# Issuing the first block of K ahead of the first query weights in a two-layer decode kernel

## The chip, the cores and the metric

The kernel runs on one core of one Trainium2 chip. The metric is device time in microseconds (us) for one execution, and a comparison of two kernels uses the median of several executions. One further execution was taken by the hardware profiler; every duration below comes from that one. Engines are called by the names of the profile: PE is the matrix engine, PEld its weight loads, DVE the vector engine, ACT the scalar engine, POOL the general one. SP is the engine that issues nearly all loads here. "SPq" stands for its queue of instructions and "ACTq" for ACT's.

## What is computed

A decode step for one token: attention over a cached K and V of 4096 positions in 32 heads of 128, then an MLP of 512 to 1376 to 512, and the same two once more with the same weights and caches. All values are 32-bit floats.

```python
def _A_ref(x, k_cache, v_cache, wq, wo):
    q = (x @ wq).reshape(B, Sq, H, Dh).transpose(0, 2, 1, 3)
    scores = jnp.einsum("bhqd,bhkd->bhqk", q, k_cache) * (Dh ** -0.5)
    p = _softmax(scores, axis=-1)
    o = jnp.einsum("bhqk,bhkd->bhqd", p, v_cache)
    return o.transpose(0, 2, 1, 3).reshape(B, Sq, H * Dh) @ wo
...
x = A_x
x = x + _A_ref(_layernorm(x), A_k_cache, A_v_cache, A_wq, A_wo)
x = x + _B_ref(_layernorm(x), B_w1, B_b1, B_w2, B_b2)
x = x + _A_ref(_layernorm(x), A_k_cache, A_v_cache, A_wq, A_wo)
x = x + _B_ref(_layernorm(x), B_w1, B_b1, B_w2, B_b2)
```

K and V hold 67 MB each, far more than the on-chip memory, so both layers stream them from device memory. A little of the second layer's data is kept over from the first.

## The kernel before

**Tiles.** The 32 heads are taken in 8 groups of 4 (`G = 8`, counted by `g`). A group's K is one block of 128 partitions x 16384 floats, 8.39 MB, loaded as one DMA (in the last group of a layer in pieces), and so is its V. Each group also has query weights (wq) and output weights (wo) of 1.05 MB each, the two of neighbouring groups loaded as one pair of 2.1 MB.

**Memory.** One tile, `arena`, holds everything that is loaded. Three homes of a block each form a ring, `RING = (0, 16 * NC, 8 * NC)`, where `NC` is 2048 floats per partition: `A_AT` at 0, `B_AT` at `16 * NC`, `C_AT` at `8 * NC`. In the first layer K of group g goes to `RING[2 * g % 3]` and V to `RING[(2 * g + 1) % 3]`: K0 to A_AT, V0 to B_AT, K1 to C_AT, V1 to A_AT again. The very first wq has no place of its own: it lies at `SHARED`, which is inside the home of V0:

```python
KEPT_V = 26 * U
SHARED = B_AT + KEPT_V
...
wq_t = by_four(load(SHARED, of_w(1, 0, 1)))
```

A block spans 32 stretches of `U = 512` floats, and wq takes stretches 26 to 29 of B_AT. So V0's load overwrites the first wq, and has to wait until that wq has landed and PE has read it. The pairs of weights that follow have their own place, `PAIR`.

**Order.** All big loads go through `load()` (line 68), which issues them from SP and keeps them in the order in which the program names them. SP executes its instructions one after the other: a load that waits holds back every load behind it. PE's instructions are kept in program order in the same way by `matmul()` (line 73). Three small loads (x, b1, b2) are issued from ACT (lines 92 to 94).

**A group in the first layer** (lines 321 to 346): load K, 32 matmuls `scores` (each shown as two records in the profile), a softmax on DVE and ACT (`exponentials`), four transposes on PE (`weights`), load V, 32 matmuls `values`, load the next pair of weights, `head_out` (output projection) and `next_queries` (the next group's queries). Ahead of the loop, `first_queries` (line 296) computes the queries of group 0: four blocks of `query_block` read wq and x, with the mean and the variance of x (`mean_of`, `rstd_of`) worked out between them. The load of K0 stands in the loop, through `blocks` (line 288), and therefore behind that of wq.

**The rest.** After group 7 come the MLP, then the second layer, which begins with the blocks still on the chip (group 7, then V of group 6) and goes down to group 0, then the second MLP and the output.

Of the kernel before, what the change touches and what calls it, by code (L numbers as in the profile page):

```python
# [23 lines left out]
C = 8  # L24
# [5 lines left out]
NC = 4 * U  # L30
# [6 lines left out]
A_AT, B_AT, C_AT = RING  # L37
# [5 lines left out]
HALVES = ((0, 4), (4, 8))  # L43
# [7 lines left out]
def decode_layers(ctx: ExitStack, tc: tile.TileContext, x, k, v, w, w1, b1, w2, b2, out):  # L51
# [5 lines left out]
    def ctile(name, *shape):  # L57
        return const.tile([P, *shape], F32, name=name)
# [6 lines left out]
    def at(first, n):  # L65
        return arena[:, first : first + n]

    def load(first, src):
        t = at(first, src.shape[-1])
        tc.keep_in_program_order(nc.sync.dma_start(t, src))  # L70
        return t
# [4 lines left out]
    def quarters(first):  # L76
        return [at(first + U * j, U) for j in range(4)]

    def part(src, g, a, b):
        return src[g][:, NC * a : NC * b]  # L80

    def of_w(row, i, n):
        return w[row][:, NC * i : NC * (i + n)]

    def by_four(t):
        return t.rearrange("p (j n) -> p j n", j=4)


    wq_t = by_four(load(SHARED, of_w(1, 0, 1)))
    b1c, b2c = ctile("b1c", FB), ctile("b2c", 4)  # L90
    xcol = ctile("xcol", 4)
# [62 lines left out]
    def idle(to, n=U):  # L154
        matmul(to[:, :n], zero[:, 0:1].to_broadcast([P, P]), at(C_AT, n), start=True, stop=True)
# [34 lines left out]
    def scores(z, c, kt):  # L190
        for j in range(J):
            matmul(pS[32 * j : 32 * j + C, :], z[:, j, C - 1 - c : 2 * C - 1 - c], kt[j],
                   start=(c == 0), stop=(c == C - 1))

    def exponentials(sc, nsc):
        nc.vector.tensor_reduce(ml[:, 0:1], pS, axis=AX.X, op=ALU.max)  # L196
        mt, m, bias = small("mt", 32), small("m"), small("mt", 32)
        nc.vector.transpose(mt, ml)
        nc.vector.tensor_reduce(m, mt[:, :C], axis=AX.X, op=ALU.max)
        nc.vector.tensor_scalar(mb[:, :C], m.to_broadcast([P, C]), nsc, None, op0=ALU.mult)  # L200
        nc.vector.transpose(bias, mb)  # L201
        p = at(SCRATCH, U)
        nc.scalar.activation(p, pS, AF.Exp, bias=bias[:, 0:1], scale=sc, accum_out=ml[:, 0:1])  # L203
        return p

    def weights(p):
        for b in range(4):
            tc.keep_in_program_order(nc.tensor.transpose(  # L208
                pT[:, b].rearrange("p j r -> p (j r)"), p[:, P * b : P * (b + 1)], ident))
        pt = work.tile([P, P], F32, name="turned").rearrange("p (j c b) -> p j c b", j=J, c=C)  # L210
        nc.vector.tensor_copy(pt, pT[:, :, :, :C].rearrange("p b j c -> p j c b"))  # L211
        lt, l, lr, rl = small("mt", 32), small("l"), small("mt", 32), small("rl")
        nc.vector.transpose(lt, ml)  # L213
        nc.vector.tensor_reduce(l, lt[:, :C], axis=AX.X, op=ALU.add)
        nc.vector.tensor_copy(lb, l.to_broadcast([P, 32]))
        nc.vector.transpose(lr, lb)
        nc.vector.reciprocal(rl, lr[:, 0:1])
        return pt, rl

    def values(i, pt, vt, c):  # L220
        for j in range(J):
            matmul(pO[32 * j : 32 * j + 4, :], pt[:, j, c, :], vt[j],
                   start=(i == 0), stop=(i == C - 1))

    def head_out(rl, wt, last=False):
        ot = at(SCRATCH, U)
        nc.vector.transpose(ot, pO)  # L227
        o, on = small("o", 4), on_wide
        own = at(SCRATCH, 4 * 129).rearrange("p (b q) -> p b q", q=129)[:, :, :P]
        own = own.rearrange("p b (d q) -> p d b q", q=32)[:, :, :, 0]  # L230
        nc.vector.tensor_reduce(o, own, axis=AX.X, op=ALU.add)  # L231
        if last:
            nc.vector.tensor_scalar(on[:, :4], o, rl, None, op0=ALU.mult)
        else:
            nc.vector.tensor_scalar(in_quarters(on, 4), o.unsqueeze(1).to_broadcast([P, J, 4]), rl, None,  # L235
                                    op0=ALU.mult)
        for d in range(4):
            if last:
                for j in range(J):
                    matmul(pS[32 * j : 32 * j + 1, :P], on[:, d : d + 1], wt[:, d, P * j : P * (j + 1)],  # L240
                           start=(d == 0), stop=(d == 3))
            else:
                matmul(pO, on[:, d : d + P], wt[:, d, :], start=(d == 0), stop=(d == 3))
        return of_32(turned(pS) if last else turned(pO, wide=True), 4)
# [34 lines left out]
    def load_w1(first, a, b):  # L279
        load(first + W1C * a, w1[:, W1C * a : W1C * b])  # L280
# [4 lines left out]
    def in_rows(first, n, rows):  # L285
        return [at(first + n * i, n) for i in range(rows)]

    def blocks(src, g, home, pieces=((0, C),)):
        for a, b in pieces:
            load(home + NC * a, part(src, g, a, b))  # L290
            for c in range(a, b):
                yield c, quarters(home + NC * c)

# [14 lines left out]
    def next_queries(n, xs, negm, wt):  # L308
        for c in range(4):
            matmul(pO, xs[:, 2 * c : 2 * c + P], wt[:, c, :], start=(c == 0), stop=(c == 3))  # L310
        return queries(n, negm, wide=True)

    def add_up(acc, own):
        t = small("acc", 4)
        nc.vector.scalar_tensor_tensor(t, own, 1.0, acc, op0=ALU.mult, op1=ALU.add)
        return t
# [4 lines left out]
    for g in range(G):  # L321
        final = g == G - 1
        k_home, v_home = RING[2 * g % 3], RING[(2 * g + 1) % 3]
        for c, t in blocks(k, g, k_home, HALVES if final else ((0, C),)):
            scores(z, c, t)
        pt, rl = weights(exponentials(sc, nsc))
        for c, t in blocks(v, g, v_home, LAST if final else ((0, C),)):
            values(c, pt, t, c)
            if final and c > 4:
                idle(pS)  # L330
            if g == G - 2:
                for j in range(J):
                    i = 4 * c + j - KEPT_V // U
                    if i >= 0:
                        nc.scalar.copy(pK[i], t[j])
        if final:
            wo_t = by_four(load(PAIR, of_w(g % 2, g, 1)))
            for i in range(3):
                load_w1(SHARED, i, i + 1)
            own = head_out(rl, wo_t, last=True)  # L340
            load_w1(SHARED, 3, 4)
        else:
            pair = load(PAIR, of_w(g % 2, g, 2))
            acc = add_up(acc, head_out(rl, by_four(pair[:, :NC])))
            wq_t = by_four(pair[:, NC:])
            z = next_queries(g + 1, xs, negm, wq_t)
# [8 lines left out]
    g = G - 2  # L355
# [28 lines left out]
    for i, first in enumerate([C_AT + 30 * U, C_AT + 31 * U] + [PAIR + U * j for j in range(4)]):  # L384
        t = at(first, U)
# [11 lines left out]
    for n in range(2, G):  # L397
        g, final = G - 1 - n, n == G - 1
        k_home, v_home = homes[(2 * n - 1) % 3], homes[2 * n % 3]
        for c, t in blocks(k, g, k_home, HALVES if final else ((0, C),)):  # L400
            scores(z, c, t)
        pt, rl = weights(exponentials(sc, nsc))
        for c, t in blocks(v, g, v_home, LAST if final else ((0, 5), (5, 8)) if n == 2 else ((0, C),)):
            values(c, pt, t, c)
            if final and c > 4:
                idle(pS)
        if final:
            wo_t = by_four(load(PAIR, of_w(g % 2, g, 1)))
            for a, b in W1_AT_END:
                load_w1(A_AT, a, b)  # L410
            for a, b in W2_AT_END:
                load_w2(A_AT + 11 * U, a, b)
            own = head_out(rl, wo_t, last=True)
        else:
            pair = load(PAIR, of_w(g % 2, g - 1, 2))
            acc = add_up(acc, head_out(rl, by_four(pair[:, NC:])))
            z = next_queries(n + 1, xs, negm, by_four(pair[:, :NC]))
# [47 lines left out]
```

## Time and profile before

| | before |
|---|---|
| median of 3 runs | 681.27 us (680.49 to 681.55) |
| the profiled execution, its own time | 679.55 us |
| its span, first to last instruction | 677.8 us |
| mean granted TensorE clock | 0.841 |
| PE busy | 433.1 us, 64% |
| DVE busy | 110.7 us, 16% |
| ACT busy | 22.2 us, 3% |
| bytes read from device memory | 286.14 MB, 422 GB/s over the span |

1.75 us of the profiled execution lie outside its span. Two things help in reading the views that follow. The page's row of DMA gives, for 40 equal slices of the span (16.9 us each), the share of time in which the 16 DMA engines were moving data, in tenths, 9 being 90% or more. The view of windows gives the same for chosen stretches, but counts each packet whole in the stretch in which it begins. A packet here is one partition's row of a load, 64 KB for a block of K or V and 8 KB for the first wq, so that in short stretches the share can be far over 1 and be followed by 0.00 while the engines are still at work on what has begun.

### The profile page before, as it was taken

The page shows a single profiled execution, that of the slowest core. Times are in us where ns is not written, and L with a number is a line of the kernel's source. Part 1 is how long each engine was busy: PE and PEld are TensorE (multiplying, and loading weights), DVE is VectorE, ACT ScalarE, POOL GpSimd, SP SyncE. Part 2 cuts the span into 40 slices and gives each one's busy share as a digit, 9 for nine tenths or more (in the row PEclk, how much of TensorE's full clock was granted, in tenths as well). Part 3 has the DMA queues.
Part 4 walks back from the last instruction along what each step waited for, and adds up shares of the span by engine and source line. Part 5 has one row for each costly group of instructions (what it writes and reads, how often), then busy time and mean ns, then how long its engine had stood idle before and what let it go on. Part 6 is the DMA issues. An engine that isn't in the chain of part 4 may idle for free. (4 is left out here: it accounts for less than half of the span.)

```text
span 677.8 us, 6359 instructions
## 1 busy us (share of the span) xinstructions
PE 433.1 (64%) x2792; PEld 119.4 (18%) x2792; DVE 110.7 (16%) x431; ACT 22.2 (3%) x47; POOL 4.3 (1%) x21
## 2 busy tenths in 40 slices
PE   1547666485554874667777897686455764766776
PEld 0112112121111211111113222221111111211112
DVE  1012101111021101210212312211021011210211
ACT  0010000000000000001000110000000000000000
POOL 1000000000000000000000000000000000000000
PEclk9969768797698876977979998998698776977977
DMA  9999999999999999999999999899999999999997
GB/s 372 434 433 433 435 433 433 416 449 437 430 433 413 451 433 430 433 431 422 428 413 359 426 459 414 358 468 441 427 433 398 465 433 423 437 430 410 426 416 294
DMA packets 11404, 286.56 MB, mean 423 GB/s; under 512 B 1776, under 2 KB 1776, under 8 KB 3440
## 3 DMA queue, kind: packets, MB, share of 16 engines
q1 hardware_dynamic: 10944, 286.14, 98.7%
q8 instruction: 22, 0.36, 0.2%
q10 hardware_dynamic: 432, 0.01, 0.0%
q14 instruction: 6, 0.05, 0.0%
HBM read 286.14 MB, written 0.00 MB: 422 GB/s over the span
## 5 line engine op out<-in xcount | busy, mean ns | idle before, releaser
L74 PE MATMUL pO<-arena,turned 128*4 128x512 f32 x1024 | 144.8, 726 | 76.8 <-DMA arena<-in_v 75.6
L74 PE MATMUL pS<-arena,zq 128*8 128x512 f32 x1024 | 137.7, 698 | 70.8 <-DMA arena<-in_k 65.4
L74 PE MATMUL pO<-arena,x_wide 128*128 128x512 f32 (+1 forms) x176 | 54.9, 508 | 24.4 <-DVE turned L137 18.1
L74 PE MATMUL pO<-arena,on_wide 128*128 128x512 f32 x112 | 51.8, 605 | 18.6 <-DVE on_wide L235 18.6
L74 PEld LDWEIGHTS pS<-arena,zq 128*8 128x8 f32 x1024 | 29.1, 99 | 176.3 <-issue 167.1
L74 PEld LDWEIGHTS pO<-arena,turned 128*4 128x4 f32 x1024 | 27.6, 97 | 183.8 <-issue 179.5
L137 DVE STREAM_TRANSPOSE turned<-pO 32x128 f32<-32x128 f32 x112 | 35.0, 312 | 101.1 <-PE pO L74 99.9
L227 DVE STREAM_TRANSPOSE arena<-pO 128x512 f32<-128x512 f32 x16 | 11.5, 717 | 220.4 <-PE pO L74 220.4
L208 PE MATMUL pO<-ident,arena 128*128 128x128 f32 x64 | 14.5, 368 | 43.9 <-ACT arena L203 42.4
L196 DVE TENSOR_REDUCE ml<-pS 128x1 f32<-128x512 f32 x16 | 11.1, 692 | 185.0 <-PE pS L74 185.0
L74 PEld LDWEIGHTS pO<-arena,x_wide 128*128 128x128 f32 (+1 forms) x176 | 21.6, 155 | 57.1 <-DVE turned L137 26.5
L203 ACT ACTIVATE arena<-pS,mt,sc 128x512 f32<-128x512 f32 x16 | 12.4, 777 | 523.7 <-DVE mt L201 523.7
L74 PEld LDWEIGHTS pO<-arena,on_wide 128*128 128x128 f32 x112 | 20.1, 189 | 51.7 <-DVE on_wide L235 31.6
L208 PEld LDWEIGHTS pO<-ident,arena 128*128 128x128 f32 x64 | 9.3, 181 | 58.6 <-ACT arena L203 51.3
L74 PE MATMUL pO<-arena,x 128*2 128x344 f32 x64 | 7.2, 531 | 5.0 <-DMA arena<-in_w 4.4
L74 PE MATMUL pS<-arena,zero 128*128 128x512 f32 x16 | 9.9, 706 | 0.0
L74 PE MATMUL pS<-arena,gelu_g 128*1 128x128 f32 x176 | 6.7, 290 | 1.5 <-DVE gelu_g L270 1.3
L213 DVE STREAM_TRANSPOSE mt<-ml 128x32 f32<-128x32 f32 x16 | 3.4, 212 | 17.2 <-ACT arena L203 17.2
L74 PEld LDWEIGHTS pS<-arena,gelu_g 128*1 128x1 f32 x176 | 3.9, 88 | 7.4 <-DVE gelu_g L270 3.7
L211 DVE COPY turned<-pO 128x128 f32<-128x128 f32 x16 | 4.4, 277 | 3.1 <-PE pO L208 3.1
L74 PE MATMUL pO<-arena,zero 128*128 128x512 f32 x8 | 4.5, 644 | 0.0
L248 POOL TENSOR_TENSOR xb<-x,b2c 128x4 f32<-128x4 f32 x2 | 0.4, 200 | 636.9 <-DVE x L148 636.9
(71 smaller groups left out, 76.5 us busy)
## 6 DMA issues: line engine op xcount, KB each, us to landing
arena<-in_w SPq DMA_DIRECT2D x13, 2048.0 KB, 28.8
arena<-in_k SPq DMA_DIRECT2D x4, 4096.0 KB, 42.5
arena<-in_v SPq DMA_DIRECT2D x2, 4096.0 KB, 47.6
arena<-in_w SPq DMA_DIRECT2D x6, 1024.0 KB, 20.3
arena<-in_v SPq DMA_DIRECT2D x1, 5120.0 KB, 23.8
arena<-in_w SPq DMA_DIRECT2D x6, 688.0 KB, 30.2
arena<-in_v SPq DMA_DIRECT2D x2, 2048.0 KB, 50.8
arena<-in_v SPq DMA_DIRECT2D x4, 1024.0 KB, 53.3
```

The lines of the kernel that those rows point to most:

```text
L74: tc.keep_in_program_order(nc.tensor.matmul(*a, **kw))
L137: nc.vector.transpose(t[q], src[q, P * j : P * (j + 1)])
L196: nc.vector.tensor_reduce(ml[:, 0:1], pS, axis=AX.X, op=ALU.max)
L203: nc.scalar.activation(p, pS, AF.Exp, bias=bias[:, 0:1], scale=sc, accum_out=ml[:, 0:1])
L208: tc.keep_in_program_order(nc.tensor.transpose(pT[:, b].rearrange("p j r -> p (j r)"), p[:, P * b : P * (b + 1)], ident))
L211: nc.vector.tensor_copy(pt, pT[:, :, :, :C].rearrange("p b j c -> p j c b"))
L213: nc.vector.transpose(lt, ml)
L227: nc.vector.transpose(ot, pO)
L248: nc.gpsimd.tensor_tensor(xb, pairs(xs)[:, :, 0], b2c, op=ALU.add)
```

## The change

One line is added ahead of the load of the first wq, which loads K0 into A_AT, and `blocks` leaves that load out when it comes to K of group 0 in the first layer. Homes, sizes, and all other loads and instructions stay as they are.

```diff
+    load(A_AT, part(k, 0, 0, C))
     wq_t = by_four(load(SHARED, of_w(1, 0, 1)))
...
-    def blocks(src, g, home, pieces=((0, C),)):
+    def blocks(src, g, home, pieces=((0, C),), first_layer=False):
         for a, b in pieces:
-            load(home + NC * a, part(src, g, a, b))
+            if src is not k or g or not first_layer:
+                load(home + NC * a, part(src, g, a, b))
...
-        for c, t in blocks(k, g, k_home, HALVES if final else ((0, C),)):
+        for c, t in blocks(k, g, k_home, HALVES if final else ((0, C),), True):
```

SP's first instructions before, with what each waits for in brackets (DMAHW1 and so on are counters of landed loads, PE_49 counts PE's work). In order these are wq of group 0, K0, V0, the first pair of weights, K1 and V1:

```order
L70 DMA arena<-in_w 128x2048
L70 DMA arena<-in_k 128x16384
L70 DMA arena<-in_v 128x16384 [waits DMAHW1_49,PE_49]
L70 DMA arena<-in_w 128x4096
L70 DMA arena<-in_k 128x16384
L70 DMA arena<-in_v 128x16384 [waits DMAHW4_49,DMAHW0_49,PE_49]
```

The same place on SP with the change:

```order
L70 DMA arena<-in_k 128x16384
L70 DMA arena<-in_w 128x2048
L70 DMA arena<-in_v 128x16384 [waits DMAHW4_49,PE_49]
L70 DMA arena<-in_w 128x4096
L70 DMA arena<-in_k 128x16384
L70 DMA arena<-in_v 128x16384 [waits DMAHW1_49,DMAHW0_49,PE_49]
```

K0 and wq have changed places, and with them their counters: DMAHW1 now counts K0 and DMAHW4 counts wq. V0 still waits for wq and for PE, and the pair and K1, which wait for nothing, still stand behind V0.

PE's first matmuls before: the four query blocks and the statistics of x (pO and pS are accumulators), then the scores of group 0 (zq holds the queries):

```order
L74 MATMUL pO<-arena,x_wide 2x128 [waits DMAHW1_49,DVE_49]
L74 MATMUL pO<-arena,x_wide 2x128 x7
L74 MATMUL pS<-x_sum,negmean 32x1 x4
L74 MATMUL pO<-arena,x_wide 2x128 x8
L74 MATMUL pS<-ss,negmean 32x1 [waits DVE_49]
L74 MATMUL pS<-ss,negmean 32x1 x3
L74 MATMUL pS<-arena,zq_93 8x512 [waits DMAHW4_49,DVE_49]
```

And with the change:

```order
L74 MATMUL pO<-arena,x_wide 2x128 [waits DMAHW4_49,DVE_49]
L74 MATMUL pO<-arena,x_wide 2x128 x7
L74 MATMUL pS<-x_sum,negmean 32x1 x4
L74 MATMUL pO<-arena,x_wide 2x128 x8
L74 MATMUL pS<-ss,negmean 32x1 [waits DVE_49]
L74 MATMUL pS<-ss,negmean 32x1 x3
L74 MATMUL pS<-arena,zq_94 8x512 [waits DMAHW1_49,DVE_49]
```

PE's order is the same. Its first matmul now waits for what is SP's second load, and its scores for what is SP's first.

## The prediction

> **What bounds the kernel now.** I read first the page's slices and its table of DMA queues, then the view of windows over the first layer, because a kernel that reads 286 MB may be limited by nothing else.
>
> ```profile
> DMA  9999999999999999999999999899999999999997
> q1 hardware_dynamic: 10944, 286.14, 98.7%
> 10.00:345.00 335.00, 199.27 (x1116) 53.00 (x1120) 48.92 (x179) 11.41 (x23) 0.00 (x0) 0.82 1.00 431
> ```
>
> The 16 DMA engines are busy in nearly every slice, and SP's queue (q1) alone fills 98.7% of their time. In the 335 us from 10 to 345 their share (the column before the last) is 1.00, at 431 GB/s, while PE is busy 199 us. So through the first layer time is bytes divided by 431 GB/s: 19.46 us for a block of 8.389 MB, 2.43 us for a wq of 1.049 MB. Where no engine has spare time, a stretch in which the DMA engines stand still is not made up later.
>
> What keeps them fed is SP. Its timeline at the start, in which the rows are wq, K0, V0, the first pair, K1 and V1:
>
> ```profile
> 0.74 0.38 SPq L70 DMA_DIRECT2D arena<-in_w  x1
> 1.18 0.42 SPq L70 DMA_DIRECT2D arena<-in_k  x1
> 8.35 0.33 SPq L70 DMA_DIRECT2D arena<-in_v  x1
> 8.72 0.43 SPq L70 DMA_DIRECT2D arena<-in_w  x1
> 9.21 0.43 SPq L70 DMA_DIRECT2D arena<-in_k  x1
> 35.11 0.33 SPq L70 DMA_DIRECT2D arena<-in_v  x1
> ```
>
> The view of DMA issues gives the time from issue to landing (last number) for wq, x, K0, V0 and K1:
>
> ```profile
> arena<-in_w SPq DMA_DIRECT2D x1, 1024.0 KB, 5.1
> xcol<-in_x ACTq DMA_DIRECT2D x1, 2.0 KB, 5.3
> arena<-in_k SPq DMA_DIRECT2D x1, 24.1
> arena<-in_v SPq DMA_DIRECT2D x1, 37.6
> arena<-in_k SPq DMA_DIRECT2D x1, 61.0
> ```
>
> wq lands at 0.74 + 5.1 = 5.84, K0 at 1.18 + 24.1 = 25.28, V0 at 8.35 + 37.6 = 45.95, K1 at 9.21 + 61.0 = 70.21. V0 is issued at 8.35, 17 us before K0 is in, so the engines go from K0's rows to V0's without a pause. That pause-free passage is what the change touches. The timeline of PE shows what released V0:
>
> ```profile
> 6.32 1.03 PE L74 MATMUL pO<-arena,x_wide 128*2 128x128 f32 x16 [6.32 <-DVE x_wide L148]
> 7.13 0.28 PE L74 MATMUL pS<-x_sum,negmean 128*32 128x1 f32 x8
> 7.25 1.03 PE L74 MATMUL pO<-arena,x_wide 128*2 128x128 f32 x16
> 8.06 0.28 PE L74 MATMUL pS<-ss,negmean 128*32 128x1 f32 x8
> 25.39 9.65 PE L74 MATMUL pS<-arena,zq 128*8 128x512 f32 x64 [17.05 <-DMA arena<-in_k]
> ```
>
> PE begins the query stage at 6.32, reads wq for the last time in the second group of 16, and V0 is issued at 8.35: 2.03 us from the stage's start to the issue. Then PE waits 17 us for K0. That wait, in which the query stage is hidden, is not a loss, because the DMA engines work through it.
>
> **The change, part by part.**
>
> *The two loads that change places.* Both orders move the same 9.437 MB from the same first issue at 0.74, so the second one lands when the second one landed: at 25.3, and it is now wq. PE began 0.11 us after K0 had landed, at 25.39, and I take the same start for the query stage. Nothing is gained at the front: K0 lands some 2.4 us earlier, but its scores need the queries, which now come after.
>
> *x.* It is loaded on ACT's queue and would have to be there too. It landed 0.2 us after the load beside it, wq. Now K0 is beside it, so I expect it near 23, ahead of wq. The cost is 0, or at worst the 0.48 us that PE took from wq's landing to its start (6.32 less 5.84), less the 0.11 counted: 0.4.
>
> *V0's wait.* The query stage is no longer beside K0's transfer. V0's issue moves to 25.39 + 2.03 = 27.42. Behind it on SP stand the pair and K1, which wait for nothing but are issued in order, so SP has nothing else to give: the engines run dry. How long an issue takes into an idle queue shows at one other place, where SP had been held up:
>
> ```profile
> 428.80 0.33 SPq L70 DMA_DIRECT2D arena<-in_v  x1
> arena<-in_v SPq DMA_DIRECT2D x1, 3072.0 KB, 9.8
> 428.50:429.70 1.20, 0.21 (x1) 0.00 (x0) 0.93 (x3) 0.00 (x0) 0.00 (x0) 1.00 0.00 0
> 429.70:430.30 0.60, 0.00 (x0) 0.00 (x0) 0.55 (x2) 0.00 (x0) 0.00 (x0) 1.00 2.81 655
> ```
>
> Issued at 428.80, no row of it begins until 429.7, and its 3.146 MB, which need 7.30 us at 431 GB/s, land after 9.8: 2.5 us over. The first wq, also into an idle queue, gives 5.1 less 2.43, or 2.7. I take 2.5, the load nearer in size. V0 then lands at 27.42 + 2.5 + 19.46 = 49.4.
>
> The Trainium skill's page "DMA: Bandwidth & Descriptors", section "Anatomy of one DMA — SWDGE (gpsimd) path", fits a load as 2.0 us fixed plus bytes at 436 GB/s. For the 3.146 MB above it would give 9.2 us where the row has 9.8, and with it V0 would land 0.7 us sooner than by my sum. It was fitted on another issuing path, and the measured row decides.
>
> *What else V0 meets.* Before, V0 landed 45.95 less 25.28, or 20.67 us after K0, 1.21 us more than its bytes need. In that stretch lies a load of instructions, seen in the view of DMA over 31 to 33 us:
>
> ```profile
> q8 instruction: 1, 0.02, 3.2%
> ```
>
> 16 KB on one of the 16 engines, 3.2% of 16 engines in 2 us, so 1.0 us, which holds up that engine's rows of V0. It came 6.5 us into the scores of K0. If it follows the program, it comes at about 34.5 now, again inside V0's transfer, and the 1.2 stay: V0 at 50.6, which is 4.6 later than 45.95. If it fell into the pause instead, the shift would be 3.4.
>
> *A second way to the same number.* The idle stretch itself:
>
> ```profile
> 24.30:24.95 0.65, 0.00 (x0) 0.00 (x0) 0.00 (x0) 0.00 (x0) 0.00 (x0) 1.00 3.76 1614
> 24.95:26.50 1.55, 1.10 (x8) 0.31 (x12) 0.00 (x0) 0.00 (x0) 0.00 (x0) 1.00 0.00 0
> ```
>
> V0's first rows begin from 24.30 to 24.95, as each engine ends its last row of K0; the zeros after them are rows under way. With the change the engines end there (middle 24.6) and the next row begins at 27.42 + 0.9 to 1.0 = 28.4: 3.8 us. The first rows after a pause run longer: of the 2.5 us, about 0.95 lie before the first row and about 0.5 between the last row and the landing (24.6 or a little later to 25.28), which leaves about 0.8 to 1.0. Together 4.6 to 4.8. I take **4.5 us** lost, with 3.4 and 5.0 (4.6 and 0.4 for x) as the ends.
>
> *How the loss reaches the end.* The scores of K0 need zq, the queries, which DVE wrote last in the query stage:
>
> ```profile
> 8.71 0.23 DVE L186 SCALAR_TENSOR_TENSOR zq<-turned,negm 128x4 f32<-128x4 f32 x1
> ```
>
> It was done at 8.94, 2.62 us after the stage's start. So the scores now begin near 28.0 instead of 25.39, and V1, which waits for them, is issued near 37.7 instead of 35.11. V0, the pair and K1 are queued by then, so this costs nothing. From V0 on, every load stands behind V0 in the queue, and PE's work on V0 waits for its landing. So loads and work move together, through the layer change as well. There the chain of waits runs over PE and DVE for a while instead of the DMA engines:
>
> ```profile
> 383.84 0.02 issue
> 387.27 7.09 PE pO L74 x64
> 399.35 7.05 PE pS L74 x64
> 410.19 8.46 PE pO L74 x64
> 430.35 7.10 PE pS L74 x64
> 441.55 8.14 PE pO L74 x64
> 460.20 47.76 DMA arena<-in_k
> ```
>
> This stretch was started by the end of the first layer, which now comes 4.5 us later; it has no input that stays where it was, so it absorbs nothing. The sum is 677.8 + 4.5 = 682.3 of span and 679.55 + 4.5 = 684.05 for the profiled execution. The median of the runs is 1.72 above that execution; against it the forecast is 681.27 + 4.5 = **685.8 us**.
>
> **The rivals.**
>
> *wq gets in ahead, no pause, not slower.* If the engines worked on wq's rows beside K0's, wq would land early, the query stage would hide beside K0 as before, and the time would stay at 681.3. It decides at wq landing by 20.8, 4.5 us before the stream's end. The Trainium skill (same page, "Queues, rings and completion order") says that completion is not in the order of issue, though each engine takes descriptors in ring order. The windows of the start speak against the rival:
>
> ```profile
> 2.90:3.40 0.50, 0.00 (x0) 0.00 (x0) 0.00 (x0) 0.00 (x0) 0.00 (x0) 1.00 1.02 410
> 5.00:5.50 0.50, 0.00 (x0) 0.00 (x0) 0.00 (x0) 0.00 (x0) 0.00 (x0) 1.00 4.35 1852
> ```
>
> K0 was issued at 1.18, but its long rows, each counted whole where it begins, show as a burst only from 5.0, when wq's are done. Rows begin strictly in the order of issue. Chance 6%, of which 2 with a small gain.
>
> *The instruction load falls elsewhere.* Then the shift is 3.4 and the time 684.7. Chance 17%.
>
> *The clock gives some back.* The V matmuls of the chain above took 7.09, 8.46 and 8.14 us. Over the slower two the granted clock (the third column from the end) was below 1:
>
> ```profile
> 410.00:415.00 5.00, 4.81 (x36) 0.96 (x40) 0.20 (x2) 0.00 (x0) 0.00 (x0) 0.70 0.98 421
> 440.00:445.00 5.00, 4.49 (x28) 1.33 (x32) 1.12 (x6) 0.08 (x1) 0.00 (x0) 0.66 1.03 441
> ```
>
> If a shifted program met the full clock there, 1.37 + 1.05 = 2.4 us would come back: 683.4. Against it: the spread of the timed runs, 680.49 to 681.55, shows how little such luck moves the total. Chance 6%, a third of it low enough to count as no change.
>
> *The pause is longer.* If PE ran its query stage at half its pace, or the chain's scores (7.05, 7.10) at the 9.65 of K0's, 2 to 5 us would be added: 687.8 and above. The query stage comes after 25 us without a matmul, but the one at 6.32 too came with no matmul before it. Chance 9%.
>
> That the change doesn't do what it says is excluded by SP's order, in which K0 stands first.
>
> **How the numbers follow.** The forecast, 685.3 to 686.3, has 62%. The range goes from 683.0 (3.4 on the lower base, 679.55) to 687.6 (5.0 on 681.55, and 1 for the clock). It leaves out the rival without a pause, most of the longer pause and some of the clock's, some 15%. About 0.2%, or 1.4 us, is what a measurement of this kernel can tell from no change. Faster by more 2% (the first rival's gain), within it 6% (4 from the first rival, 2 from the clock's), slower by more 92%.
>
> **What would show it.** Right: V0's issue at 27.4, the query stage of PE at 25.4 with wq as its releaser, windows without any new row from about 25 to 28.3, V0 landing at 49.4 to 50.6, all later issues of SP 3.4 to 4.6 later by about the same amount, and no change of rate in between. Wrong: V0 issued before 24, which would mean that wq came in beside K0; an issue near 27.4 and a V0 that lands less than 3 us later than before; or a shift that is there at 300 us and smaller after 460, which would mean that the layer change took it up.

## The result and the profile after

The change made the kernel slower: 686.13 us (median of 6 runs, 684.6 to 687.24) against 681.0 (6 runs, 680.19 to 681.55). The ratio is 1.0082, with a 95% interval of 1.0068 to 1.0096, or 4.6 to 6.5 us. The profiled execution took 687.24 us, at the upper end of its runs, with a span of 685.4, and the one before (679.55) lies below its six runs; the excess of one profile over the other, 7.6 us of span, is therefore more than the change itself.

The page of the kernel after, its slices and its main DMA queue:

```profile
DMA  9799999999999999999999999899999999999997
q1 hardware_dynamic: 10944, 286.14, 97.9%
```

One digit has fallen from 9 to 7: the second slice, from 17 to 34 us. The bytes are the same.

SP's timeline at the start of the kernel after (start, duration, instruction), in the order K0, wq, V0, pair, K1, V1:

```profile
0.73 0.37 SPq L70 DMA_DIRECT2D arena<-in_k  x1
1.16 0.42 SPq L70 DMA_DIRECT2D arena<-in_w  x1
27.76 0.33 SPq L70 DMA_DIRECT2D arena<-in_v  x1
28.14 0.43 SPq L70 DMA_DIRECT2D arena<-in_w  x1
28.62 0.42 SPq L70 DMA_DIRECT2D arena<-in_k  x1
37.25 0.33 SPq L70 DMA_DIRECT2D arena<-in_v  x1
```

V0 is issued at 27.76 instead of 8.35, and the pair and K1 follow it at once: they had only been queued behind it. The view of DMA issues gives the times to landing of K0, x, wq and V0:

```profile
arena<-in_k SPq DMA_DIRECT2D x1, 22.3
xcol<-in_x ACTq DMA_DIRECT2D x1, 2.0 KB, 22.5
arena<-in_w SPq DMA_DIRECT2D x1, 1024.0 KB, 24.4
arena<-in_v SPq DMA_DIRECT2D x1, 23.9
```

K0 lands at 23.0, x at 23.2, wq at 25.56, V0 at 27.76 + 23.9 = 51.66. PE's timeline at the start of the query stage and at K0's scores:

```profile
25.74 1.03 PE L74 MATMUL pO<-arena,x_wide 128*2 128x128 f32 x16 [25.74 <-DMA arena<-in_w]
28.47 8.71 PE L74 MATMUL pS<-arena,zq 128*8 128x512 f32 x64 [0.70 <-DVE pS L175]
```

The view of windows of the same kernel (share and GB/s of the rows that begin are the last two columns):

```profile
24.95:26.50 1.55, 0.76 (x16) 0.60 (x20) 0.00 (x0) 0.00 (x0) 0.00 (x0) 1.00 0.00 0
26.50:28.50 2.00, 1.30 (x44) 0.89 (x40) 1.08 (x8) 0.00 (x0) 0.21 (x1) 1.00 0.00 0
28.50:29.00 0.50, 0.50 (x4) 0.09 (x8) 0.13 (x2) 0.00 (x0) 0.34 (x1) 1.00 3.70 1180
```

Between 24.95 and 28.50 not one row begins. Before, the zeros after 24.95 were rows of V0 under way, 64 KB each; here the last rows were wq's of 8 KB, so the engines really stand still while PE runs the query stage. A good place to compare the two later is the load of the weights of groups 6 and 7, at the end of the first layer. In SP's timeline before it stands at 284.20:

```profile
284.20 0.33 SPq L70 DMA_DIRECT2D arena<-in_w  x1
```

And after, at 289.12:

```profile
289.12 0.33 SPq L70 DMA_DIRECT2D arena<-in_w  x1
```

That issue comes 4.92 us later. It is a rough measure, because SP waits for PE there and PE's pace varies (the V matmuls ahead of it took 9.57 us before and 9.23 after): the issues of SP that stood at 124, 152, 168, 210 and 254 us before come 5.1, 6.8, 4.9, 6.6 and 4.9 later. The stream itself shows where PE waits for a block to land. K of group 7, the last of the layer, in PE's timeline before:

```profile
288.73 9.40 PE L74 MATMUL pS<-arena,zq 128*8 128x512 f32 x64 [4.56 <-DMA arena<-in_k]
```

And after:

```profile
293.99 9.06 PE L74 MATMUL pS<-arena,zq 128*8 128x512 f32 x64 [4.89 <-DMA arena<-in_k]
```

So the first layer's stream runs 5.26 us later, from a pause in its first 30 us.

### The profile page after: what moved, and what is told of

Same layout as the page of the kernel before. It is cut to its first block, busy times and chain, and to the rows that moved or that the text cites. A ratio compares the mean times of both kernels' runs of the same rounds, so it can differ in the third digit from the quotient of the medians.

```text
span 685.4 us, 6359 instructions
## 1 busy us (share of the span) xinstructions
PE 429.6 (63%) x2792; PEld 118.9 (17%) x2792; DVE 110.2 (16%) x431; ACT 22.2 (3%) x47; POOL 4.3 (1%) x21
## 5 line engine op out<-in xcount | busy, mean ns | idle before, releaser
L209 PE MATMUL pO<-ident,arena 128*128 128x128 f32 x64 | 12.5, 327 | 43.9 <-ACT arena L204 42.4
L209 PEld LDWEIGHTS pO<-ident,arena 128*128 128x128 f32 x64 | 7.9, 160 | 58.6 <-ACT arena L204 51.3
L388 ACT COPY arena<-pK 128x512 f32<-128x512 f32 x6 | 3.4, 587 | 32.0 <-PE pS L74 16.5
```

The lines of the kernel that those rows point to most:

```text
L209: tc.keep_in_program_order(nc.tensor.transpose(pT[:, b].rearrange("p j r -> p (j r)"), p[:, P * b : P * (b + 1)], ident))
L388: nc.scalar.copy(t, pK[i])
```

## The experiments

**The theory** is the pause: every us by which V0's issue comes too late to join K0's transfer is lost. **Rival 1** is that the queries, and with them the scores of K0, come 3 us later. **Rival 2** is the start itself: rows of 64 KB first, and x landing at 23 instead of 6. Where the order is not the change's, the diff is against the kernel before. What a comparison gives in us is its ratio times 681.

**K0 first, wq elsewhere** (against the change):

```diff
-    wq_t = by_four(load(SHARED, of_w(1, 0, 1)))
+    wq_t = by_four(load(PAIR, of_w(1, 0, 1)))
```

> K0 first as in the change, but the first wq lies in PAIR, outside the home of V0, so that V0's load waits for nothing. Theory (the pause): the loss comes from the DMA engines standing still while V0's load waits for wq's readers; V0 is now issued near 1.6 us, no windows without new rows at 25 to 28.5, and the time is back at 681.0, within 0.8. Rival 1 (late queries): the loss comes from the scores of K0 starting 3 us later; they start as late here, so 685 to 686. Rival 2 (the start with 64 KB rows, x landing at 23): also unchanged here, 685 to 686.

Measured: 681.06 us against 681.1, ratio 1.0003 (0.9989 to 1.0017). The timeline of this kernel, of SP first and then of PE:

```profile
0.74 0.38 SPq L70 DMA_DIRECT2D arena<-in_k  x1
1.18 0.42 SPq L70 DMA_DIRECT2D arena<-in_w  x1
1.65 0.42 SPq L70 DMA_DIRECT2D arena<-in_v  x1
28.11 0.33 SPq L70 DMA_DIRECT2D arena<-in_w  x1
...
28.82 7.89 PE L74 MATMUL pS<-arena,zq 128*8 128x512 f32 x64 [0.71 <-DVE pS L175]
```

The scores begin even later than with the change, 28.82, and x comes as late, but V0 is issued at 1.65 and the loss is gone. Both rivals fall. The wait has passed to the pair (28.11), where some 17 us of V0 are still to be moved (PE begins on V0 at 46.17) and nobody misses it.

**wq first, wq elsewhere** (the same edit on the kernel before):

> The kernel before (wq first) with the first wq in PAIR: the control for the other place. The pause theory: V0's load already had no pause, so nothing changes, 681.0 within 0.8. Both rivals: the same. If the other place costs or gains something by itself, it shows here, and is to be taken off the first experiment.

Measured: 681.4 us against 681.1, ratio 1.0000 (0.9988 to 1.0012). The place by itself costs nothing and gains nothing, within 0.8 us.

**wq first, V0 late:**

```diff
             scores(z, c, t)
+            if g == 0 and c == 0:
+                matmul(pK[0][:2, :P], pairs(xs)[:, 0, :], wq_t[:, 0, :P], start=True, stop=True)
```

> The kernel before (wq first, queries early) with one matmul of 128 columns added behind the first 4 of K0's 32 scores matmuls, which reads wq again and writes an accumulator bank that nothing reads; so V0's load waits for K0. Pause theory: the scores begin at 25.4, V0 is issued at about 27.0, 0.8 earlier than with the change (27.76), and the loss is the 4.9 seen there less 0.8, or 4.1: 685.1, within 0.8. Rivals 1 and 2: queries early, start as before, so 681.0 to 681.3.

Measured: 686.4 us against 681.1, ratio 1.0070 (1.0054 to 1.0087), or 3.7 to 5.9 us. The pause alone, in the old order and with early queries, costs what the change costs, as far as the two intervals tell. The four score matmuls ahead of the added one took longer than I had allowed. The timeline of this kernel, of PE first and then of SP:

```profile
25.38 1.90 PE L74 MATMUL pS<-arena,zq 128*8 128x512 f32 x8 [17.07 <-DMA arena<-in_k]
27.04 0.42 PE L74 MATMUL pK<-arena,x_wide 128*2 128x128 f32 x1
...
27.70 0.33 SPq L70 DMA_DIRECT2D arena<-in_v  x1
```

V0 left at 27.70 and not at 27.0, which is the change's own time to within 0.1; so the miss in the expected number (685.1), 0.7 by the ratio and 1.3 by the medians, is at least in part the 0.7 of the issue time.

**The change, with the query stage's matmuls doubled** (`first_queries` gets the parameter `again`, and the call of the first layer passes `True`):

```diff
+        if again:
+            for c in range(4):
+                for j in range(J):
+                    matmul(pK[0][32 * j : 32 * j + 2, :P], pairs(xs)[:, c, :], wt[:, c, P * j : P * (j + 1)],
+                           start=(c == 0), stop=(c == 3))
         z = queries(0, negm)
```

> The change, with the 16 query matmuls done a second time into an accumulator bank that nothing reads, ahead of the last matmuls of the query stage. It lengthens the stage by about 1.6 us (2.0 less the 0.3 of the two small groups). Pause theory: V0 is issued at about 29.4, and each us of later issue costs one: 686.1 + 1.6 = 687.7, within 0.8. Rival 1: the scores start 1.6 later too, so up to the same if late queries count in full, but V1's issue is covered by 40 us of queue, so it would show no idle windows. Rival 2: 686.1, no change.

Measured: 687.56 us against 681.1, ratio 1.0087 (1.0069 to 1.0105). V0 is issued at 29.73, 2.0 later than with the change. Against the change and its repeat the medians differ by 1.1 to 1.4 us, the ratios by only 0.3 to 0.5, and the intervals overlap, so the time does not show the step. The trace agrees with it: the load that stood at 289.12 stands at 291.23, and K of group 7, which reached PE at 293.99, reaches it at 295.69.

**K0 in two parts around wq**, six eighths first, and seven eighths first (against the change; `n` is 6 or 7):

```diff
-    load(A_AT, part(k, 0, 0, C))
+    load(A_AT, part(k, 0, 0, n))
     wq_t = by_four(load(SHARED, of_w(1, 0, 1)))
+    load(A_AT + NC * n, part(k, 0, n, C))
```

> As the change, but only six eighths of K0 go ahead of the first wq and the last two eighths (2.1 MB, 4.9 us) follow it; wq stays inside V0's home. Pause theory: wq lands 4.9 us ahead of the end of K0, at about 20.7, the query stage ends and V0 is issued at about 22.9, just before the engines end K0's last rows (24.6 less the 1.0 from issue to first row): no pause or one below 0.4, 681.1 to 681.5. If late loads of x or a start with long rows counted, it would stay at 685 to 686.

Measured: 681.46 us against 680.9, ratio 1.0004 (0.9992 to 1.0015).

> The same with seven eighths ahead of wq and one (1.05 MB, 2.4 us) behind it. Pause theory: wq lands 2.4 earlier than with the change, V0 is issued at about 25.3 instead of 27.7, so 2.4 of the 5.1 us come back: 683.7, within 0.8. A threshold without a slope would show 681 or 686.

Measured: 683.93 us against 680.9, ratio 1.0040 (1.0022 to 1.0058). V0's issue in SP's timeline of the first of the two, with six eighths ahead:

```profile
23.30 0.33 SPq L70 DMA_DIRECT2D arena<-in_v  x1
```

And of the second, with seven eighths ahead:

```profile
25.40 0.33 SPq L70 DMA_DIRECT2D arena<-in_v  x1
```

Both times came as the theory had them, and the issues 0.4 and 0.1 later than expected. As far as these runs resolve it, order matters only through the time at which V0 leaves.

**The change again:**

> The change, unaltered, for a second profile. In the first one SP's issues are 4.9 us later than before up to 328 us and 7.6 later after 437, with V matmuls of 8.79, 8.79 and 8.51 us at the layer change where before had 7.09, 8.46 and 8.14. If the further 2.7 us belong to the clock that this one execution was granted, the shift after 437 is now nearer to 5, and the time is 686.1 within 0.6. If they belong to the change, the shift grows by 2 to 3 us at the layer change again.

Measured: 686.46 us against 680.9, ratio 1.0079 (1.0066 to 1.0091). Here the load at the end of the first layer stands at 288.76, 4.56 later than before, and the issue of V that stood at 437.46 before stands at 444.14, 6.7 later (in the first profile of the change 445.08, 7.6 later). The shift grew by 2 us again, which I had taken as the sign that the change does it, but in another place. The chain of waits has the first V matmuls of the second layer as follows in the first profile of the change:

```profile
392.88 8.79 PE pO L74 x64
```

And in this one:

```profile
393.65 7.09 PE pO L74 x64
```

In the first, these 64 records took 1.70 more than in the profile before (7.09) and most of the growth came there. In the second they took just as long as before, and its growth lies earlier, in the matmuls of the MLP. The granted clock (third column from the end of the view of windows) shows what the two have in common. The V matmuls, before and in the first profile of the change:

```profile
387.27:394.40 7.13, 7.05 (x64) 1.61 (x64) 0.01 (x1) 0.00 (x0) 0.00 (x0) 1.00 0.99 426
392.88:401.70 8.82, 8.74 (x64) 1.85 (x64) 0.01 (x1) 0.00 (x0) 0.00 (x0) 0.81 0.97 415
```

The stretch of the MLP up to the next issue of K, before and in the repeat:

```profile
362.18:369.39 7.21, 6.13 (x79) 2.48 (x80) 1.52 (x6) 0.21 (x1) 0.00 (x0) 1.00 0.92 336
367.36:375.76 8.40, 8.27 (x79) 2.97 (x80) 1.53 (x6) 0.21 (x1) 0.00 (x0) 0.71 0.86 297
```

Both times the same matmuls ran longer, by 1.70 and 1.19, where the granted clock was lower. So most of the growth is the clock's, as in my first explanation, though a second execution met it too.

All kernels together, by the time at which V0 leaves. The first shift is that of the load which stood at 284.20 before, in each one's profile; the second is that of PE's start on K of group 7, which stood at 288.73; the ratio has its interval in brackets:

| kernel | V0 issued | shift at 284 us | shift of K at 289 us | ratio of times |
|---|---|---|---|---|
| wq first, wq elsewhere | 1.63 | 0.17 | -0.03 | 1.0000 (0.9988 to 1.0012) |
| K0 first, wq elsewhere | 1.65 | 0.30 | 0.71 | 1.0003 (0.9989 to 1.0017) |
| six eighths of K0 first | 23.30 | 0.91 | 0.47 | 1.0004 (0.9992 to 1.0015) |
| seven eighths first | 25.40 | 2.63 | 2.70 | 1.0040 (1.0022 to 1.0058) |
| wq first, V0 late | 27.70 | 5.23 | 5.43 | 1.0070 (1.0054 to 1.0087) |
| the change | 27.76 | 4.92 | 5.26 | 1.0082 (1.0068 to 1.0096) |
| the change again | 27.98 | 4.56 | 5.47 | 1.0079 (1.0066 to 1.0091) |
| stage doubled | 29.73 | 7.03 | 6.96 | 1.0087 (1.0069 to 1.0105) |

From 23.30 on, a us of later issue costs about a us of the first layer's stream: by the shift of K, 1.1 from the first split of K0 to the second, 1.1 from there to the change, 0.9 from the change to the doubled stage, whichever edit made it late. The two rows on top, which lost no time, show what a single profile scatters: 0.0 and 0.7.

**The same finding at another place.** In the kernel before, SP is held up once more at 428.80, by the second piece of a V block, with a pair of weights behind it whose place is free. The pair goes ahead (against the kernel before; the old load of the pair is left out for this group):

```diff
             values(c, pt, t, c)
+            if n == 2 and c == 4:
+                pair = load(PAIR, of_w(g % 2, g - 1, 2))
```

> The kernel before, with the same finding used at another place: in the second layer SP waits until 428.80 for the second piece of V of group 5, and the pair of weights (2.1 MB, 4.9 us) that stands behind it has its place free at 418.6. The pair is issued ahead of that piece. Pause theory: the engines, which ran dry from about 427.6 to 429.7 and restarted with slow first rows, work on the pair then; V's second piece lands near 440, before PE begins V at 441.6. Gain 2.0 to 2.6: 678.5 to 679.1. If a pause there is covered (the chain of waits runs over PE from 384 to 460), no change: 681.1.

Measured: 679.82 us against 680.9, ratio 0.9988 (0.9978 to 0.9998), a gain of 0.1 to 1.5 us. The sign is right and the size is less than half. SP's timeline of this kernel, the pair and then the second piece of V:

```profile
418.78 0.33 SPq L70 DMA_DIRECT2D arena<-in_w  x1
428.80 0.33 SPq L70 DMA_DIRECT2D arena<-in_v  x1
```

Its view of DMA issues, the second piece with the time to landing:

```profile
arena<-in_v SPq DMA_DIRECT2D x1, 3072.0 KB, 14.7
```

Its view of windows, at the old pause:

```profile
428.50:429.70 1.20, 0.27 (x1) 0.00 (x0) 0.87 (x3) 0.00 (x0) 0.00 (x0) 1.00 0.93 389
```

The window that had no new row before is at 0.93, so the pause is gone. Why that brought so little shows in the profile before. Its view of DMA issues for the first piece of V, which was issued at 406.36:

```profile
arena<-in_v SPq DMA_DIRECT2D x1, 5120.0 KB, 23.8
```

And its window ahead of the pause:

```profile
427.50:428.50 1.00, 1.00 (x3) 0.19 (x1) 0.00 (x0) 0.00 (x0) 0.00 (x0) 1.00 0.26 98
```

That piece landed at 406.36 + 23.8 = 430.16, after the first rows of the next one had begun (from 429.7). In the last window with new rows the share is 0.26, or 4.2 us of rows in 1 us for 16 engines: most began nothing more. Taken one by one from the trace, the rows of the 16 engines end between 427.58 and 429.74, half of them by 428.1, and the next rows begin from 429.76. A landing counts the slowest engine. The pause was 2.2 us long for the first engine and nothing for the last, and so its end gains little. In the new kernel the lag stays: the second piece lands at 428.80 + 14.7 = 443.5, where I had expected 440.

The stream does gain at first. PE's start on K of the next group is 1.54 earlier, before and then in this kernel:

```profile
464.49 8.56 PE L74 MATMUL pS<-arena,zq 128*8 128x512 f32 x64 [4.74 <-DMA arena<-in_k]
462.95 8.75 PE L74 MATMUL pS<-arena,zq 128*8 128x512 f32 x64 [3.15 <-DMA arena<-in_k]
```

And on the first piece of the last V, 200 us on:

```profile
648.69 6.90 PE L74 MATMUL pO<-arena,turned 128*4 128x512 f32 x48 [2.34 <-DMA arena<-in_v]
648.68 6.89 PE L74 MATMUL pO<-arena,turned 128*4 128x512 f32 x48 [3.92 <-DMA arena<-in_v]
```

There the gain is gone in this pair of profiles: half of the engines end that piece by 645.31 instead of 646.90, but the last one ends it at 648.04 against 648.05. I read this from one execution of each kernel and did not test it apart; why the last engine lags so far there stays open. This version is faster than the kernel before by a margin just clear of no change, and so than the change.

## Why the prediction was right, point by point

- **The bound.** Right. The stream of loads was full, and nothing later made the pause good: in the first profile PE's starts on landed blocks came 5.1 to 5.6 us later through the first layer, in the repeat 5.2 to 5.5, and more in the second. The sign that I had named, SP's issues 3.4 to 4.6 later, was set too low: after the first layer they came 5.6 to 7.8 later in the first profile.
- **What the change moves.** Right. K0's earlier landing (23.0 instead of 25.3) brought nothing, x landed at 23.2 as expected and held nobody up (PE was released by wq), and the wait moved onto V0, with the pair and K1 behind it.
- **V0's issue.** 27.42 was forecast, 27.76 measured (27.98 in the repeat). The query stage took 2.02 us, as taken (2.03). The term that was off is its start: I had taken 25.39, the start of PE after K0 before, and it was 25.74, 25.95 and 26.0 in the profiles of the change, its repeat and the doubled stage. wq landed at 25.56 and not at 25.28, so "the second one lands when the second one landed" was 0.3 off, and PE started 0.18 behind it instead of 0.11.
- **The landing of V0.** 50.6 was forecast, 51.66 measured. Of the 1.06 us, 0.34 is the late issue; from issue to landing it took 23.9 where the sum had 2.5 + 19.46 + 1.2 = 23.2. In the repeat it took 23.2 and V0 landed at 51.18. Both are past the 50.6 that I had named as the latest. The pause itself was forecast as 3.8 us, from 24.6 to 28.4; by the rows of the trace the engines ended at 24.67 and began V0 at 28.95 (medians of the 16), so it was 4.3. The rest of the stream kept the shift: K of group 7 came 5.26 later in the first profile and 5.47 in the repeat, against 4.5 for the forecast.
- **The total.** 4.5 forecast, 5.1 measured by the medians, 5.6 by the ratio and 5.4 by the repeat's, inside the range of 683.0 to 687.6. So the mechanism was right and its size 0.6 to 1.1 too small: 0.3 to 0.6 is the later issue, and 0.1 to 0.3 I gave away myself, since my two sums had come to 4.6 and to 4.6 to 4.8 and I took 4.5. That 685.8 lies only 0.3 from 686.13 is partly luck: the median before had been 681.27 in three runs and is 681.0 in six.
- **The layer change.** I had said that this stretch absorbs nothing; nor did it, but it isn't neutral either. Both profiles of the change gained some 2 us at SP's issues there (2.2 and 0.7 by PE's starts, from the last V of the first layer to the first K of the second that PE waits for), each in matmuls at a granted clock below that of the profile before (0.81 and 0.71 against 1.00). The kernel with V0 late and the one with the doubled stage, with pauses as long, did not gain (from 284 to 437 their shifts go from 5.23 to 5.23 and from 7.03 to 7.40). A single profile carries luck of that size, and the medians, at 5.1 to 5.6, hardly leave room for it beside the 5.3 to 5.5 of the first layer. Whether this order of loads makes the lower clock more likely is not settled.
- **The rivals.** wq getting in ahead did not happen: it was issued at 1.16 and landed after K0. The load of instructions that could have fallen into the pause came inside V0's transfer, as forecast: between 35 and 37 us in the first profile, between 33 and 35 in the repeat. A longer pause in PE's stage did not happen either: the query stage took 2.02 us and K0's scores 8.71. That the clock would give back 2.4 us at the layer change was wrong in sign for these executions.

## What to carry to other kernels

When one queue issues all loads in order and the stream is the bound, ask of every load which waits how many us of transfers are still ahead of it at that moment; as long as that is more than the wait, the wait is free, and once it is less, every us is lost, for all the loads behind as well. A small load whose consumer releases a large one belongs well ahead of the end of the stream, or in a place that no later load needs. A pause is worth removing only by what it costs the slowest DMA engine; in the one pair of profiles here that was much less than the view of windows shows.

## What the hardware showed that I had not expected

- A small load landed with the large one beside it: x, 2 KB on ACT's queue, took 5.3 us beside the 1 MB of wq and 22.5 beside the 8.4 MB of K0.
- The 16 DMA engines drift apart: they ended the piece of V above between 427.58 and 429.74, and restarted within 0.5 us of each other, from 429.76 to 430.23. Such a pause lets the slow engine catch up, which would hide a part of the pause's cost; these figures are of one place in one profile.
